# Fifteen unread one-element instructions behind the early sums of a fused decode layer

## The chip, the cores and the metric

The kernel runs on one core of a Trainium2 chip. The metric is the device time of one execution in microseconds (us). A core has five engines, each with a program of its own: TensorE (PE in the profile, PEld for its weight loads), VectorE (DVE), ScalarE (ACT), GpSimd (POOL) and SyncE (SP). [...] An engine's queue is written with a q (DVEq); instructions there, such as semaphore waits and DRAINs, are not counted as busy.

## What is computed

One decode step for 4 sequences with model width 1024, in bf16: a layer norm, grouped-query attention over the last 2048 positions of a key and value cache (32 query heads, 4 key and value heads of 128), a residual, a second layer norm, and a gated feed-forward block of width 3584 with a second residual.

```python
def reference(A_x, A_k_cache, A_v_cache, A_wq, A_wo, B_x, B_w1, B_w3, B_w2):
    x = A_x
    h = x + _A_ref(_layernorm(x, axis=-1), A_k_cache, A_v_cache, A_wq, A_wo)
    ...
    def _B_ref(x, w1, w3, w2):
        gate = jnp.einsum("bsd,df->bsf", x, w1)
        up = jnp.einsum("bsd,df->bsf", x, w3)
        h = _silu(gate) * up
        out = jnp.einsum("bsf,fd->bsd", h, w2)
        return out
    ...
    return h + _B_ref(_layernorm(h, axis=-1), B_w1, B_w3, B_w2)
```

## The kernel before

All weights and the two caches stream from HBM once, through SP's queue, into one large SBUF buffer, `ring` (line 96), whose five units are used over again. The order of the work is written out by hand (`manual_schedule`, line 134): each engine runs its instructions in the order of the program text, and the framework adds the semaphore waits. SBUF tiles that are allocated later lie behind those allocated earlier in the same pool; `ring` lies behind the pool `act`.

The stages are: layer norm of x and the query projection (to line 259); transposes of the keys and the scores (lines 277 to 434); softmax and the weighted values (to line 453); the output projection, whose residual sum lands in `h1`, 128 partitions of 256 numbers (lines 455 to 497); the second layer norm; gate and up projections (line 505 on); and the down projection with `w2`, which ends the kernel.

The down projection is cut in two by the order in which `w2` arrives. The early part multiplies the first 21 of 28 row groups and one part of the last into `early_ps` (function `early`, L560, and L583). Then VectorE adds `early_ps` to `h1` in two sums, one for each half of the partitions (L596); these are the two early sums of the title. The late part multiplies the remaining groups into three accumulators `y2_ps` (function `late`, L608). One matmul (L627) carries a part of `h1` into the second of them. The end is:

- ScalarE copies a piece of the result out of PSUM (L641) and VectorE adds two others to `h1` (L642 and L646). Each of L642 and L646 waits for its early sum and for TensorE.
- SP and ScalarE send two pieces each to HBM (L651).
- The closing block of the program, all on L679: SP waits for the output DMAs and for the last count of each engine's semaphore. Then come two barriers. In each, every engine but GpSimd executes a DRAIN that also counts up a gather semaphore, and then waits for a release; GpSimd executes a DRAIN of its own, waits for the four reports and releases all. Between the two barriers GpSimd clears the semaphores (EVENT_SEMAPHORE_RANGE_CLEAR). A DRAIN starts only when the release semaphore of the barrier before is back at zero. The opening block (L668) has one such barrier.

Ahead of the change GpSimd's last instruction is L542, a product for the last row group, and VectorE's are the two sums of L596.

Of the kernel before, what the change touches and what calls it, by code (L numbers as in the profile page):

```python
# [10 lines left out]
P = 128  # L11
# [4 lines left out]
FP32 = mybir.dt.float32  # L16
# [5 lines left out]
def kernel(  # L22
# [20 lines left out]
    nc = tc.nc  # L43
# [41 lines left out]
    act = ctx.enter_context(tc.tile_pool(name="act", bufs=1))  # L85
# [56 lines left out]
    for b in range(B):  # L142
# [19 lines left out]
        out=same[:], in_=t32[:].rearrange("p (o h) -> p o h", o=1).to_broadcast([P, C, R])  # L162
# [16 lines left out]
        out=asel[:].rearrange("p a y -> p y a"), in0=fold2[:, :, 0], in1=fold2[:, :, 1], op=ALU.add  # L179
# [3 lines left out]
    for j in range(JM):  # L183
# [3 lines left out]
        out=nscale[:], in_=ident_f[:2, :2], scalar=-qscale, op=ALU.mult  # L187
# [5 lines left out]
        out=place[:, : R * C].rearrange("p (h e) -> p h e", e=C)[:, :, C - 1], in_=t32[:]  # L193
# [6 lines left out]
        out=gather[:, :, :B], in_=ident[:].rearrange("p (c b s) -> p c b s", c=C, b=B)[:, :, :, 0]  # L200
# [60 lines left out]
    for r in range(REP):  # L261
# [8 lines left out]
        out=Qm[:].rearrange("p b (g y) -> p b g y", y=QW)[:, :, :, :REP],  # L270
        in_=qT_ps[:, :, :, :B].rearrange("p r g b -> p b g r"),
# [223 lines left out]
    h1 = act.tile([P, DQ], FP32)  # L495
# [42 lines left out]
    for hf in range(2):  # L538
# [4 lines left out]
        out=last_m[:],  # L543
# [50 lines left out]
    for k in range(2):  # L594
        part = h1[2 * R * k : 2 * R * k + 2 * R, :]
        nc.vector.tensor_tensor(out=part, in0=early_ps[:, k], in1=part, op=ALU.add)  # L596

    y2_ps = [
        ps.tile(shape, FP32, tag=tag, name="y2_ps")
        for shape, tag in (([P, DH], "scA"), ([P, DH], "ktB"), ([P, DQ], "scB"))  # L600
# [37 lines left out]
    for k in range(2):  # L638
        part = slice(2 * R * k, 2 * R * k + 2 * R)
        if k == 0:  # L640
            nc.scalar.copy(out=res[part, DH:], in_=y2_ps[1][part, :])  # L641
            nc.vector.tensor_tensor(  # L642
                out=res[part, :DH], in0=y2_ps[0][part, :], in1=h1[part, :DH], op=ALU.add
            )
        else:
            nc.vector.tensor_tensor(  # L646
                out=res[part, :], in0=y2_ps[2][part, :], in1=h1[part, :], op=ALU.add
            )
        for i, eng in enumerate((nc.sync, nc.scalar)):
            c = 2 * k + i  # L650
            eng.dma_start(  # L651
                out=out_flat[:, c * DQ : (c + 1) * DQ], in_=res[R * c : R * c + B, :]
# [31 lines left out]
```

## Time and profile before

| | us |
|---|---|
| median of 3 runs (lowest to highest) | 138.51 (138.48 to 138.62) |
| the profiled execution | 138.48 |
| its span, first to last instruction | 136.7 |
| TensorE busy | 80.7 (59%) |
| VectorE busy | 48.6 (36%), 45 instructions |
| GpSimd busy | 17.7 (13%), 50 instructions |
| HBM read | 55.58 MB, 407 GB/s over the span |

Times inside the profile are counted from the start of the span. Where a record is given to the thousandth, it is read from the trace's own start and length of that instruction; the views print starts to a tenth or a hundredth. A line of the groups reads: line, engine, operation, output and input with shapes, count, then busy us and mean ns of one, then the idle time of the engine just before and what ended it. Matmul ends are modelled, and GpSimd's spans are rough.

### The profile page before, as it was taken

What the parts mean: (1) busy time and instruction counts of PE and PEld (TensorE: products, weight loads), DVE (VectorE), ACT (ScalarE), POOL (GpSimd) and SP (SyncE); (2) the same over time, 40 slices, a digit from 0 to 9 for tenths busy, and PEclk for the clock granted to TensorE, in tenths of its full rate; (3) what the DMA queues carried; (4) which work ended last, traced back from release to release, by engine and by line L of the source; (5) the groups of instructions that cost most, each with busy time, mean ns of one, the idle gap of its engine ahead of it and who ended that gap; (6) DMA issues with size and microseconds to landing.
All of it is one profiled execution on the core that took longest, in us unless ns stands there. A gap on an engine that the chain in (4) does not pass through costs nothing.

```text
span 136.7 us, 1804 instructions
## 1 busy us (share of the span) xinstructions
PE 80.7 (59%) x779; PEld 43.5 (32%) x779; DVE 48.6 (36%) x45; ACT 29.9 (22%) x35; POOL 17.7 (13%) x50
## 2 busy tenths in 40 slices
PE   0000044959999985129992993995198000999770
PEld 0000022449966941023332340541043000444440
DVE  0000110007625463899299922001100297062022
ACT  3000140027959495013000000002501700000100
POOL 7600061000000000000084633000300000001000
PEclk9999999999999999855698699999856855569998
DMA  4999697999999999998978979969899798999960
GB/s 168 525 420 538 269 537 307 436 417 446 417 422 441 412 432 422 417 590 360 556 326 384 537 326 475 520 285 537 352 453 508 302 520 364 397 414 423 403 235 2
DMA packets 2782, 55.69 MB, mean 407 GB/s; under 512 B 312, under 2 KB 600, under 8 KB 728
## 3 DMA queue, kind: packets, MB, share of 16 engines
q1 hardware_dynamic: 2740, 55.58, 95.3%
q8 instruction: 6, 0.10, 0.3%
q10 hardware_dynamic: 36, 0.01, 0.0%
HBM read 55.58 MB, written 0.01 MB: 407 GB/s over the span
## 4 chain that ended last, share of the span: by engine, by line
DMA 56%; PE 30%; DVE 6%; ACT 3%; SPq 1%; issue 1%; DVEq 0%
DMA ring<-in_B_w_dram 40%; DMA ring<-in_A_wq_dram 16%; PE kt_ps L283 9%; PE sc_ps L306 5%; PE o_ps L397 5%; PE gate L510 4%; PE q_ps L249 4%; DVE P L360 2%; DVE PT L382 2%; SPq L128 1%; ACT ring L287 1%; PE small L397 1%; DVE ring L285 1%; DVE rmax L318 1%; ACT q_sb L259 1%
## 5 line engine op out<-in xcount | busy, mean ns | idle before, releaser
L287 ACT COPY ring<-kt_ps 128x2048 bf16<-128x2048 bf16 x8 | 14.6, 1866 | 7.1 <-PE kt_ps L283 7.1
L283 PE MATMUL kt_ps<-ident,ring 128*128 128x128 bf16 x256 | 15.0, 219 | 0.6 <-DVE Qm L269 0.5
L283 PEld LDWEIGHTS <-ring 128*128 128x128 bf16 x256 | 14.4, 98 | 2.6 <-issue 1.7
L414 POOL TENSOR_TENSOR o<-od 128x256 f32<-128x256 f32 x4 | 6.8, 1696 | 55.5 <-DVE od L405 55.5
L285 DVE COPY ring<-kt_ps 128x2048 bf16<-128x2048 bf16 x8 | 9.8, 1225 | 9.3 <-PE kt_ps L283 9.3
L510 PE MATMUL up<-ring,n_T 128*32 128x448 bf16 x64 | 6.0, 568 | 10.9 <-DMA ring<-in_B_w_dram 10.9
L209 PE MATMUL sums_ps<-both,mean_f 128*128 128x64 f32 x4 | 1.1, 366 | 19.0 <-ACT both L207 19.0
L397 PE MATMUL o_ps<-ring,PT 128*128 128x512 bf16 x32 | 11.5, 541 | 0.0
L510 PEld LDWEIGHTS <-n_T 128*32 128x32 bf16 x128 | 5.1, 143 | 20.3 <-DMA ring<-in_B_w_dram 11.5
L397 PEld LDWEIGHTS <-PT 128*128 128x128 bf16 x64 | 7.6, 121 | 10.3 <-issue 5.7
L532 DVE RECIPROCAL eg<-eg 128x896 f32<-128x896 f32 x1 | 5.8, 5753 | 10.9 <-ACT eg L531 10.9
L360 DVE TENSOR_TENSOR P<-p,gmask 128x2048 bf16<-128x2048 bf16 x4 | 9.1, 2278 | 0.8 <-ACT p L347 0.8
L382 DVE STREAM_TRANSPOSE PT<-P 128x2048 bf16<-128x2048 bf16 x4 | 9.2, 2306 | 0.1
L249 PE MATMUL q_ps<-ring,n_T 128*32 128x512 bf16 x64 | 6.2, 556 | 3.6 <-DMA ring<-in_A_wq_dram 1.8
L306 PE MATMUL sc_ps<-ring,Qm 128*32 128x512 bf16 x64 | 7.6, 605 | 0.4 <-DVE ring L285 0.4
L510 PE MATMUL gate<-ring,n_T 128*32 128x448 bf16 x64 | 5.9, 558 | 3.0 <-DMA ring<-in_B_w_dram 3.0
L397 PE MATMUL small<-ring,PT 128*128 128x512 bf16 x32 | 7.2, 379 | 0.0
L484 PE MATMUL y_ps<-ring,oP 128*32 128x512 bf16 x64 | 7.1, 379 | 0.1
L209 PEld LDWEIGHTS sums_ps<-both,mean_f 128*128 128x128 f32 x4 | 0.8, 249 | 19.4 <-issue 17.1
L234 DVE STREAM_TRANSPOSE x_T<-x_nat 128x256 bf16<-128x256 bf16 x1 | 0.6, 626 | 15.9 <-DMA x_nat<-in_A_x_dram 15.9
L560 PE MATMUL early_ps<-ring,hg_T 128*32 128x512 bf16 x42 | 5.0, 379 | 1.1 <-DMA ring<-in_B_w_dram 1.1
L464 ACT CAST oP<-on_ps 128x128 bf16<-128x128 f32 x1 | 0.3, 266 | 22.6 <-PE on_ps L457 22.6
(94 smaller groups left out, 68.9 us busy)
## 6 DMA issues: line engine op xcount, KB each, us to landing
ring<-in_B_w_dram SPq DMA_DIRECT2D x2, 7168.0 KB
ring<-in_A_k_cache_dram SPq DMA_DIRECT2D x4, 2048.0 KB, 25.6
ring<-in_A_v_cache_dram SPq DMA_DIRECT2D x4, 2048.0 KB, 42.8
ring<-in_A_wq_dram SPq DMA_DIRECT2D x1, 7168.0 KB, 21.2
ring<-in_B_w_dram SPq DMA_DIRECT2D x1, 3328.0 KB
ring<-in_B_w_dram SPq DMA_DIRECT2D x1, 2048.0 KB, 23.3
ring<-in_A_wq_dram SPq DMA_DIRECT2D x1, 1024.0 KB, 4.5
ring<-in_B_w_dram SPq DMA_DIRECT2D x1, 1024.0 KB
```

The lines of the kernel that those rows point to most:

```text
L249: nc.tensor.matmul(q_ps[R * c : R * c + R, hf], lhsT=xn_T[:, kc, :], rhs=wq_s[:, kc, o : o + HALF * Dh], start=(kc == 0), stop=(kc == KC - 1),
L283: nc.tensor.transpose(out=kt_ps[:, jj], in_=blocks[:, jj, :], identity=ident[:])
L285: nc.vector.tensor_copy(out=blocks, in_=kt_ps[:])
L287: nc.scalar.copy(out=blocks, in_=kt_ps[:])
L306: nc.tensor.matmul(sc_ps[b // 2][R * q : R * q + R, b % 2], lhsT=Qm[:, b, g * R : (g + 1) * R], rhs=kT[:, b, g, q], start=(g == 0), stop=( ...
L360: nc.vector.tensor_tensor(out=P4[:], in0=stage.pop(("p1", b))[:].rearrange("p (x o) -> p x o", o=1).to_broadcast([P, JR * L5, Hkv]), in1=g ...
L382: nc.vector.transpose(out=PT[:].rearrange("p j h -> p (j h)"), in_=stage.pop(("P4", b))[:].rearrange("p x g -> p (x g)"),)
L397: nc.tensor.matmul(o_ps, lhsT=PT[:, i * JM : (i + 1) * JM, :].rearrange("p j h -> p (j h)"), rhs=v_s[b][:, i * JM : (i + 1) * JM, :], star ...
L414: nc.gpsimd.tensor_tensor(out=o2[:], in0=od[:, :2], in1=od[:, 2:], op=ALU.add)
L484: nc.tensor.matmul(y_ps[R * i : R * i + R], lhsT=oP[:, t, :], rhs=row[:, i], start=False, stop=(t == T - 1), tile_position=(0, R * i), ski ...
L510: nc.tensor.matmul(out_ps[hf][R * c : R * c + R, :], lhsT=hn_T[:, kc, :], rhs=cols[:, kc, c, hf], start=(kc == 0), stop=(kc == KC - 1), ti ...
L532: nc.vector.reciprocal(out=eg[:], in_=eg[:])
```

## The change

Two tiles of 128 by 8 fp32 are allocated in the pool `act`, one for each engine. Behind the two early sums GpSimd copies one element of `h1` into its tile, and then seven further elements of each tile are set to zero, VectorE writing its own and GpSimd its own. Nothing reads the two tiles. Lines behind the insertion have numbers higher by 7: L642 becomes L649, L646 becomes L653, L679 becomes L686.

```diff
@@ -595,6 +595,13 @@
         part = h1[2 * R * k : 2 * R * k + 2 * R, :]
         nc.vector.tensor_tensor(out=part, in0=early_ps[:, k], in1=part, op=ALU.add)
 
+    pad_v = act.tile([P, 8], FP32)
+    pad_p = act.tile([P, 8], FP32)
+    nc.gpsimd.tensor_copy(out=pad_p[:1, :1], in_=h1[:1, :1])
+    for i in range(1, 8):
+        nc.vector.memset(pad_v[:1, i : i + 1], 0.0)
+        nc.gpsimd.memset(pad_p[:1, i : i + 1], 0.0)
+
     y2_ps = [
         ps.tile(shape, FP32, tag=tag, name="y2_ps")
         for shape, tag in (([P, DH], "scA"), ([P, DH], "ktB"), ([P, DQ], "scB"))
```

In the built programs VectorE has 67 instructions in the body in place of 60 and GpSimd 62 in place of 54; TensorE, ScalarE and SP have as many as before, in the same order with the same waits. The one new wait is that of GpSimd's copy for the second early sum; SP's closing wait asks for 54 counts of GpSimd's semaphore in place of 46. The seven memsets of VectorE stand ahead of the waits of L649 in its program. The buffer `ring` starts 64 bytes higher in each partition, as does `res`, the tile of the result.

## The prediction, made before the result was known

> **What bounds the kernel now.** I read the page's chain first, then the timeline of the last 6 us, then the records of the closing line L679, which the chain leaves out. The chain says that the weight stream sets the pace:
>
> ```profile
> DMA 56%; PE 30%; DVE 6%; ACT 3%; SPq 1%; issue 1%; DVEq 0%
> ```
>
> The change lies behind the last big wait on that stream. The timeline from 131 us (start, length, engine, line; in brackets the idle time before it and what ended it):
>
> ```profile
> 131.04 0.87 DVE L596 TENSOR_TENSOR h<-early_ps,h 64x256 f32<-64x256 f32 x2 [7.06 <-PE early_ps L560]
> 131.61 0.63 PE L608 MATMUL y_ps<-ring,hg_T 128*32 128x128 bf16 x24 [0.60 <-DMA ring<-in_B_w_dram]
> ...
> 132.17 0.43 PE L627 MATMUL y_ps<-h,ident_f 128*64 128x128 f32 x2
> ...
> 132.88 0.62 PE L608 MATMUL y_ps<-ring,hg_T 128*32 128x128 bf16 x14 [0.28 <-DMA ring<-in_B_w_dram]
> 133.26 0.28 DVE L642 TENSOR_TENSOR res<-y_ps,h 64x128 bf16<-64x128 f32 x1 [1.35 <-PE y_ps L608]
> ...
> 133.58 0.43 DVE L646 TENSOR_TENSOR res<-y_ps,h 64x256 bf16<-64x256 f32 x1
> ```
>
> The two early sums (L596) end at 131.91. VectorE then stands idle for 1.35 us, until TensorE's late products, which themselves wait for the last weights, release L642. GpSimd does nothing after L542 ends at 124.68.
>
> The span ends at 136.69, 2.7 us after L646. Output DMAs take it to 135.64; then come two closing barriers, in which every engine reports with a DRAIN, GpSimd gathers the reports, and all are released. The records of L679 from 135.6 to 136.8 (engine's queue, count, ns min/median/max, first and last start):
>
> ```profile
> L679 SPq DRAIN  x2: 7/7/7, 135.6 to 135.9; - x2
> ...
> L679 POOLq DRAIN  x2: 39/58/78, 135.8 to 136.1; - x2
> L679 ACTq DRAIN  x1: 8/8/8, 135.9 to 135.9; - x1
> L679 POOLq EVENT_SEMAPHORE_RANGE_CLEAR  x1: 96/96/96, 135.9 to 135.9; - x1
> L679 PEldq DRAIN  x1: 13/13/13, 136.0 to 136.0; - x1
> L679 DVEq DRAIN  x1: 143/143/143, 136.3 to 136.3; - x1
> ```
>
> All four other engines are released by the first barrier at about 135.80. SP starts its next DRAIN 75 ns after its release has ended, ACT 74, PE 98; VectorE needs 496 ns (135.825 to 136.321), and its DRAIN lasts 143 ns where VectorE's own DRAIN at the program's start took 10. GpSimd has finished its own duties at 136.107, and its gather comes at 136.498, 34 ns behind the end of VectorE's DRAIN (136.464). So **VectorE holds up the last barrier**, by 0.35 us over what GpSimd would need (136.107 + 0.044, the spacing of GpSimd's DRAIN and gather in the opening barrier, is 136.15). Nothing that the trace records as a wait explains this: the semaphore that the DRAIN asks to be zero is zero when PE's release ends, 135.855, and SP and ACT pass at once.
>
> **My reading of it.** The late instruction is a place in VectorE's program rather than a kind of work. Instructions reach the engines in pieces, as page part 3 shows:
>
> ```profile
> q8 instruction: 6, 0.10, 0.3%
> ```
>
> That is 0.10 MB in 6 packets, some 16 KB each, during the span, for the engine with the long program. VectorE's built program has 3 instructions in the opening block, 60 in the body and 4 at the end; the slow one is the 66th, the second closing DRAIN. I take it that a boundary between pieces lies there and costs 0.43 + 0.13 = 0.56 us (the late start over 75 ns, the long DRAIN over 10 ns). That is an inference: the trace holds one such place on VectorE.
>
> [...]
>
> **The change part by part.**
>
> *Removed and moved.* Nothing is taken out. TensorE, ScalarE and SP keep their instructions and waits in the same order. On VectorE all that follows L596 moves 7 places down: the 66th instruction is now the semaphore wait ahead of the first result sum (L642, now L649), right behind the last memset. The boundary, if it is one, is then passed in the 1.35 us of idle time, and the closing DRAIN is an ordinary one. VectorE would report at 135.825 + 0.09 + 0.01 = 135.93, GpSimd gathers at 136.15 in place of 136.498: **-0.35 us**. What is late next is GpSimd itself.
>
> *Seven memsets on VectorE.* The trace has no memset on VectorE. The nearest rows:
>
> ```profile
> L341 DVE COPY bias<-small 128x2 f32<-128x2 f32 x2 | 0.3, 133 | 1.3 <-PE small L333 1.3
> L378 DVE RECIPROCAL rinv<-small 128x2 f32<-128x2 f32 x2 | 0.3, 131 | 0.0
> ...
> L184 POOL MEMSET jmask<- 32x1 f32 x4 | 0.4, 91 | 0.2
> ...
> L668 POOL MEMSET const-float32-0.0<- 128x1 f32 x1 | 0.1, 98 | 0.2 <-issue 0.2
> ```
>
> Upper end: 133 ns and the 31 ns between the two L596 make 164, times 7 is 1.15 us. Lower end: GpSimd's four opening memsets start 34 ns apart, times 7 is 0.24. I take the same kind of operation's length, 98 ns: 0.69 us, from 131.91 to 132.60. Add 0.56 for the boundary: 133.16, before TensorE's release at 133.24. So **0 us**. The spare time is only 0.08 us, but VectorE's sequencer runs ahead: L642's first wait is recorded at 131.497, during the second L596, so the stall can begin while the memsets still run. At the upper end VectorE would be ready at 133.62, 0.36 us late, which eats the whole gain; at the lower it has 0.5 us to spare. Neither TensorE's L627 nor anyone else waits for the memsets.
>
> *Eight instructions on GpSimd.* The copy waits for the second L596 and reads one element of its result. The smallest such rows take 200 ns (L171, L199). Seven memsets start 34 ns apart (L668) to 128 ns (L184): 0.24 to 0.90. From 131.94 they end between 132.4 and 133.05. Behind them GpSimd has only the closing barrier, whose first gather waits for SP at 135.64: 2.6 us of cover, so **0 us**. SP's closing wait asks for eight more counts from GpSimd, long there.
>
> *Do the two disturb one another?* The rows that bear on it are GpSimd's sums beside a busy and beside an idle VectorE:
>
> ```profile
> 68.94 2.70 POOL L414 TENSOR_TENSOR o<-od 128x256 f32<-128x256 f32 x1 [47.97 <-DVE od L405]
> ...
> 80.67 0.73 POOL L414 TENSOR_TENSOR o<-od 128x256 f32<-128x256 f32 x1 [3.32 <-DVE od L405]
> ```
>
> The first runs beside VectorE's L360 (68.77 to 71.05), the second alone: GpSimd lost 2 us, VectorE nothing (L360 took 2.28 us there and 2.29 without GpSimd). So GpSimd yields, and it has cover.
>
> [...]
>
> *Memory.* The two pads push the weight buffer up by 64 bytes in each partition; packet sizes stay. No row prices this. A tenth of a percent of the 136.7 us of streaming would be 0.14 us either way; I take 0.
>
> **Sum.** The profiled execution took 138.48 us, 1.79 more than its span, and lies 0.03 below the median 138.51. 138.48 - 0.35 = 138.13, or 138.16 against the median: I say **138.15**.
>
> **The rivals.**
>
> *No change.* VectorE's late DRAIN belongs to the closing sequence itself (whatever comes second there is late) and moves along. For it: a single observation, and none of VectorE's 65 earlier instructions can be seen to stall, though most lie behind longer waits. Against it: no other engine is late at that step, and VectorE's opening DRAIN took 10 ns. Everything added is covered: 138.5.
>
> *Slower: the boundary lands in a worse place.* If the real boundary lies up to 7 places past the 66th, today it falls behind the span's last release; moved 7 up, it falls in the closing barriers, where VectorE is already last, at up to 0.56 us: 139.05. Or the memsets cost so much that the stall ends past 133.24. That decides from 0.11 us per memset on, and outweighs the saving from about 0.16. At that upper end the first result sum is 0.36 us late and the gain is gone; only beyond it is the change a loss. For it: each late step of VectorE now has something ahead of it. Against: the late DRAIN sits where a boundary would show.
>
> *Slower: GpSimd holds VectorE up.* Should all 15 run one after another at upper prices, 1.15 + 0.2 + 0.9 = 2.25 us from 131.91 is 134.16, 0.9 us past 133.26, less 0.35 at the end or not: 139.0 to 139.4. The L414 rows speak against it.
>
> *GpSimd has a late place of its own* between 136.107 and 136.464, now hidden, and its 8 instructions fail to move it away: the gain shrinks to below 0.2, counted as no change.
>
> **How the numbers follow.** About 0.2% (0.28 us) is what a measurement of this kernel can tell from no change. Forecast (faster by 0.25%): 0.50, a little of it falling below that line by the memsets' price, against some chance that more is saved in the 1.79 us outside the span. No change, with the shrunken gain: 0.28. The boundary in a worse place: 0.16; GpSimd holding VectorE: 0.06. So faster 0.50, same 0.28, slower 0.22. The forecast's own range is 137.95 to 138.30 (0.35 with the 0.14 of the buffer's shift); the range of all, to 138.85, takes in no change and the milder losses, and leaves out some 0.15.
>
> **What would show it.** Right: VectorE's last DRAIN starts within 0.1 us of its release, lasts some 10 ns, and the gather follows GpSimd's own DRAIN; the memsets end before 132.7; the first result sum still starts 20 to 30 ns after TensorE's last FIRST product. Wrong: the DRAIN is as late as before (no change), L649 starts later against TensorE than 0.03 us (boundary or memsets too dear), or the closing barriers grow. The forecast fails as a whole if the delay follows the closing sequence and not the count of instructions.

## The result, and the profile after

The changed kernel is **slower by 0.51%** (ratio 1.0051, 95% interval 1.0032 to 1.0070): median 139.15 us over 14 executions (138.78 to 140.12) against 138.63 (138.48 to 138.80). The prediction was 138.15. Seven of the 14 lie at 138.97 or below and seven at 139.33 or above, and the median is the middle between the two groups; the profiled one took 138.93, with a span of 137.12 where the span before was 136.69.

The end of the timeline of the changed kernel (start, length, engine, line, in brackets the idle time and what ended it):

```profile
129.94 1.90 PE L560 MATMUL early_ps<-ring,hg_T 128*32 128x512 bf16 x16 [1.71 <-DMA ring<-in_B_w_dram]
...
131.88 0.87 DVE L596 TENSOR_TENSOR h<-early_ps,h 64x256 f32<-64x256 f32 x2 [8.06 <-PE early_ps L560]
132.36 0.18 POOL L600 COPY pad_p<-h 1x1 f32<-1x1 f32 x1 [7.85 <-DVE h L596]
...
132.48 0.29 POOL L603 MEMSET pad_p<- 1x1 f32 x7
132.80 0.11 DVE L602 MEMSET pad_v<- 1x1 f32 x7
...
133.67 0.61 PE L615 MATMUL y_ps<-ring,hg_T 128*32 128x128 bf16 x14 [0.28 <-DMA ring<-in_B_w_dram]
...
134.06 0.28 DVE L649 TENSOR_TENSOR res<-y_ps,h 64x128 bf16<-64x128 f32 x1 [1.15 <-PE y_ps L615]
```

Three things are to be seen. The fifteen instructions are short and covered: VectorE's seven take 0.11 us, GpSimd's eight 0.41, and VectorE still waits for TensorE before L649. Everything is late *before* they start: the early sums begin at 131.88 where they began at 131.04. And what came late is a weight load: TensorE waited 1.71 us for its rows ahead of 129.94. Before the change the same products stood here:

```profile
129.10 1.90 PE L560 MATMUL early_ps<-ring,hg_T 128*32 128x512 bf16 x16 [0.76 <-DMA ring<-in_B_w_dram]
```

The closing barrier, on the other hand, is as short as predicted. The records of the closing line from 136.7 to 136.97:

```profile
L686 DVEq DRAIN  x1: 19/19/19, 136.7 to 136.7; - x1
...
L686 POOLq DRAIN  x1: 34/34/34, 136.9 to 136.9; - x1
L686 POOLq EVENT_SEMAPHORE  x1: 17/17/17, 136.9 to 136.9; - x1
```

VectorE's last DRAIN now starts 90 ns after its release and lasts 19 ns (496 and 143 before); the last gather follows GpSimd's own DRAIN. From the first release to the last gather it is 0.38 us in place of 0.73. So the account of the profiled execution is **+0.79 us** on the weight stream, **-0.35** at the closing barrier, together +0.44; the spans differ by 0.43.

What is new in the page is one row of part 3. The rows behind the weight queue's, before and after:

```profile
q8 instruction: 6, 0.10, 0.3%
q10 hardware_dynamic: 36, 0.01, 0.0%
```

```profile
q8 instruction: 6, 0.10, 0.3%
q10 hardware_dynamic: 36, 0.01, 0.0%
q14 instruction: 2, 0.02, 0.0%
```

Two pieces of program, 8 KB each, are now fetched inside the span. The list of packets has them at 103.37 and 120.08 us; before, two such packets came at 136.99 and 137.18, behind the span's end. The weight queue and the fetch in the window 119.8 to 121 (packets, MB, share of 16 engines):

```profile
q1 hardware_dynamic: 22, 0.59, 116.9%
q14 instruction: 1, 0.01, 1.7%
```

Here is how so small a packet can matter. Each of the large loads lands in 16 parts, which I read as one for each of the core's 16 DMA engines (no view names the engine of a part), and TensorE starts behind the last: the parts of the 8 rows land by 129.06 before and by 129.90 after, the products on them start at 129.10 and 129.94. The landing times of the parts, from the trace, in us after the first part of the same load (13 rows of w2 at 122.3, then 8 rows at 127.2; between them lies the small load of 128 KB for the last row group, L524):

```
            13 rows: early parts   late parts            8 rows: late parts
before      11, 0.00 to 0.50       1.71 1.80 1.83 1.86 1.86           nine, 1.62 to 1.87
after       9, 0.00 to 0.36        0.73 1.25 1.59 ... 1.77 (five)     1.54 ... 1.77 (seven), 2.20, 2.74
```

Five parts are late by 1.59 us or more at 122 in both kernels: by then five 16 KB pieces have been fetched (the packets of queue 8, which I take for TensorE's, the engine with the long program: 779 products and 779 weight loads; no view names the engine). The small load makes four more late. In the changed kernel two further parts stand out at 122, by 0.73 and 1.25, and behind the small load they stand at 2.20 and 2.74: **they gained another 1.47 and 1.49**. So, if a part is a DMA engine, each fetch fell on one that the small load makes late as well, and the delays added up. The four parts of the small load itself show the same: before, they land within 0.12 us of one another; after, two of them land 0.67 and 1.20 us behind the first (with VectorE's instructions alone, in the experiments, one of the four does, by 1.23; with GpSimd's alone one, by 0.65). The later loads keep that order, and the last part of the last 512 KB load lands at 133.63 in place of 132.84.

### The profile page after: what moved, and what is told of

It reads as the page before. It is cut to its first block, busy times and chain, and to the rows that moved or that the text cites. A ratio compares the mean times of both kernels' runs of the same rounds, so it can differ in the third digit from the quotient of the medians.

```text
span 137.1 us, 1817 instructions
## 1 busy us (share of the span) xinstructions
PE 80.1 (58%) x777; PEld 43.3 (32%) x779; DVE 48.8 (36%) x52; ACT 29.9 (22%) x35; POOL 18.2 (13%) x58
## 4 chain that ended last, share of the span: by engine, by line
DMA 56%; PE 30%; DVE 6%; ACT 3%; SPq 1%; issue 1%; DVEq 0%
DMA ring<-in_B_w_dram 41%; DMA ring<-in_A_wq_dram 15%; PE kt_ps L283 9%; PE sc_ps L306 5%; PE o_ps L397 4%; PE gate L510 4%; PE q_ps L249 4%; DVE P L360 2%; DVE PT L382 2%; SPq L128 1%; ACT ring L287 1%; PE small L397 1%; DVE ring L285 1%; DVE rmax L318 1%; ACT q_sb L259 1%
```

## The experiments

My theory (A in the texts below) was now: the longer programs of VectorE and GpSimd have their next piece fetched during the stream, and the fetch makes one DMA engine late. The rivals were the weight buffer's 64 bytes (B), and the instructions themselves (C). All kernels allocate the two tiles, and the diffs below are against the changed kernel, unless the text says otherwise.

### One engine at a time

```diff
-    nc.gpsimd.tensor_copy(out=pad_p[:1, :1], in_=h1[:1, :1])
     for i in range(1, 8):
         nc.vector.memset(pad_v[:1, i : i + 1], 0.0)
-        nc.gpsimd.memset(pad_p[:1, i : i + 1], 0.0)
```

> Both tiles allocated, VectorE's seven memsets kept, GpSimd's eight instructions left out. Theory A (an engine whose program grows past a boundary fetches its next piece of program during the weight stream, and the fetch holds up the one DMA engine that carries it): one packet of 8 KB on queue 14 inside the span in place of two, VectorE's second closing DRAIN starts within 0.1 us of its release and lasts some 20 ns, the last weights land either as before (time 138.25) or up to 0.8 us late (139.0). Theory B (the 64-byte shift of the weight buffer slows the stream): as slow as the whole change less nothing, 139.0 to 139.2, with no packet needed. Theory C (the 15 instructions disturb each other or the end): about 138.6.

```diff
     for i in range(1, 8):
-        nc.vector.memset(pad_v[:1, i : i + 1], 0.0)
         nc.gpsimd.memset(pad_p[:1, i : i + 1], 0.0)
```

> Both tiles allocated, GpSimd's eight instructions kept, VectorE's memsets left out. Theory A: one packet on queue 14 inside the span, VectorE's closing DRAIN as late as before (0.5 us after its release, 143 ns long), so the end saves nothing; time 138.6 if the fetch falls on a DMA engine with time to spare, up to 139.4 if not. Theory B: 139.0 to 139.5. Theory C: about 138.6.

VectorE alone: 139.60 us (ratio 1.0064, 1.0043 to 1.0085). GpSimd alone: 138.91 (1.0036, 1.0018 to 1.0055). Each has one packet in the stream, so the fetches can be told apart: VectorE's is the one at 120 us, GpSimd's the one at 101 to 103. The queue's row in the window 119.8 to 121 of VectorE alone, then in 101 to 102 of GpSimd alone:

```profile
q14 instruction: 1, 0.01, 1.7%
```

```profile
q14 instruction: 1, 0.01, 1.9%
```

The last part of the 512 KB load lands at 133.62 and 133.19. VectorE alone was dearer than expected, because its closing barrier saves nothing: GpSimd has a late place of its own. The closing line from 137.25 to 137.85 in that kernel:

```profile
L684 POOLq DRAIN  x1: 39/39/39, 137.4 to 137.4; - x1
L684 POOLq EVENT_SEMAPHORE  x1: 17/17/17, 137.8 to 137.8; - x1
```

VectorE has reported at 137.24, yet GpSimd gathers 0.40 us after its own DRAIN (137.415 to 137.813), where the opening barrier needs 0.044. Before the change that was hidden behind VectorE, but with nothing to spare: there GpSimd's gather stood 0.39 us behind its own DRAIN too (136.107 to 136.498). So there were two late places that ended together. From the first release to the last gather it is 0.73 us before, 0.74 with VectorE's instructions alone, 0.74 with GpSimd's alone (there VectorE's DRAIN is the late one, 126 ns long), and 0.38 only with both.

### The tiles without instructions, and the instructions in another place

```diff
     pad_v = act.tile([P, 8], FP32)
     pad_p = act.tile([P, 8], FP32)
-    nc.gpsimd.tensor_copy(out=pad_p[:1, :1], in_=h1[:1, :1])
-    for i in range(1, 8):
-        nc.vector.memset(pad_v[:1, i : i + 1], 0.0)
-        nc.gpsimd.memset(pad_p[:1, i : i + 1], 0.0)
```

> The two tiles are allocated and nothing is done with them: the weight buffer starts 64 bytes higher, the programs are those of before. Theory A: 138.6, no packet on queue 14 inside the span, closing DRAIN as late as before. Theory B: 139.0 to 139.5, the last weights land 0.4 to 0.8 us later. Theory C: 138.6.

The other kernel has the seven and the eight ahead of the first transpose, at line 238, and nothing behind the early sums (against the kernel before):

```diff
+    pad_v = act.tile([P, 8], FP32)
+    pad_p = act.tile([P, 8], FP32)
+    for i in range(1, 8):
+        nc.vector.memset(pad_v[:1, i : i + 1], 0.0)
+    for i in range(8):
+        nc.gpsimd.memset(pad_p[:1, i : i + 1], 0.0)
+
     x_T = act.tile([P, KC, R], BF16, tag="xT")
```

> As many instructions as in the whole change (seven memsets on VectorE, eight on GpSimd), but at the head of the kernel, where VectorE waits 15 us for its first input and GpSimd prepares constants; none stands behind the early sums. Theory A (the count decides, not the place): two packets on queue 14 inside the span, a short closing DRAIN on VectorE, the same time as the whole change within 0.3 us (138.8 to 139.5). Theory B: the same 139.0 to 139.5. Theory C (disturbance at the end): 138.6 or below.

The tiles alone: 138.43 us, ratio 0.9985 (0.9977 to 0.9994), no packet, closing DRAIN late as before. The 64 bytes cost nothing; this kernel is a little faster than the one before: B falls. At the head: 138.96 (1.0040, 1.0022 to 1.0059), two packets (103.5 and 118.0 us), a short closing DRAIN: C falls too. **With these counts it is the number of instructions that decides, not their place.**

### The small load over all DMA engines

```diff
-    load(w2_a, w2_v[:, FC - 1, :HD].rearrange("(y a) n -> a y n", a=C))
+    load(w2_a, w2_v[:, FC - 1, :HD].rearrange("(p t) n -> p t n", p=PA))
```

> The whole change, and the small load of the last row group (128 KB, which goes to HBM's and SBUF's sides in 4 outer rows and was carried by 4 of the 16 DMA engines) written with 16 outer rows, so that all 16 carry it; the rows then lie in another order, so a small part of the last group's products is not the reference's. Theory A (each of the two fetches falls on a DMA engine that the small load makes late as well, and the two delays add up): two packets on queue 14 inside the span, but no part of the last loads stands out by more than 0.3 us; the last weights land at most 0.4 us later than in the spread kernel without the fifteen instructions, or at the same time, and this kernel is 0.3 to 0.4 us faster than that one by the shorter closing barrier: about 138.3 to 138.6. Theory D (a fetch costs the stream its delay whatever else its DMA engine carries): 0.4 to 0.8 us slower than that kernel, 139.2 or more.

> The two tiles alone, none of the fifteen instructions, and the small load of the last row group over all 16 DMA engines as in the kernel beside it (the same part of the output is not the reference's). Theory A: no packet on queue 14 inside the span, VectorE's closing DRAIN late; the DMA engines that carried TensorE's program pieces are late by their 1.3 us and now by some 0.3 us of the small load too, so the last weights land 0.2 to 0.4 us later than with the tiles alone: 138.6 to 138.8. Theory D: the same.

With the fifteen instructions 139.77 us (1.0089, 1.0076 to 1.0102), without them 140.16 (1.0123, 1.0097 to 1.0148). The order is that of A, and so is the distance: 0.39 us faster with them by the medians, though the two intervals just overlap. The last part of the 512 KB load lands at 134.50 with and 134.54 without, so two fetches in the stream (101.4 and 119.1 us) cost nothing there, and from the first release to the last gather it is 0.38 us with and 0.74 without. D falls. The level was missed by 1.2 and 1.4 us: with 16 outer rows the small load, whose target is still only 16 partitions, made *every* part of the loads behind it about 1.7 us later, where with four it made four parts 1.5 us later. Why, these runs do not show.

That 4 outer rows mean 4 DMA engines, and 16 all of them, is my reading. The trace has the number: before the change the small load lands in 4 parts (123.91 to 124.03 us), and behind it nine parts of a large load are late in place of five. Which engines carry a fetch, no view here names, but by the late parts of the small load they are among its four.

### How the late place moves with the count

```diff
     nc.gpsimd.tensor_copy(out=pad_p[:1, :1], in_=h1[:1, :1])
-    for i in range(1, 8):
+    for i in range(1, v + 1):
         nc.vector.memset(pad_v[:1, i : i + 1], 0.0)
+    for i in range(1, p):
         nc.gpsimd.memset(pad_p[:1, i : i + 1], 0.0)
```

Here v is the number of memsets on VectorE and p that of GpSimd's instructions, the copy included; the kernels write the same instructions out or in another order of the two engines, and each engine's own order is this one. With v = 3, p = 4, and with v = 1, p = 1:

> Three memsets on VectorE and four instructions on GpSimd in place of seven and eight. If both programs pass the boundary with so few: two packets on queue 14 inside the span and the time of the whole change, 138.8 to 139.9. If one passes: one packet, 138.9 to 139.6. If neither: no packet, 138.4 to 138.6, or 138.1 if the closing DRAIN is short all the same, which my prediction's count of places allows (the late place would then fall behind the last result sum, where VectorE waits for the first closing release).

> One memset on VectorE and the one copy on GpSimd. If a boundary is passed by so little: packets on queue 14 inside the span as above, 138.8 or more. If not: 138.4 with the closing DRAIN as late as before, or 138.1 with a short one (by the count of places, the late place would fall on VectorE's wait for the first closing release, where 1.7 us are free).

3 and 4: 139.36 us (1.0058, 1.0046 to 1.0070). 1 and 1: 138.63 (1.0004, 0.9996 to 1.0013). No packet comes in the stream in either, the last weights land as with the tiles alone (132.74, 132.70; there 132.78), and the late place sits where the count puts it. With one memset VectorE's closing DRAIN is short (24 ns, 135.81), but GpSimd's one instruction brings its late place onto its last DRAIN (371 ns after the clearing, 176 long; the last gather at 136.53), where nothing hides it. With three VectorE's falls on the second result sum, which starts 0.23 us behind the first, and GpSimd's on the first release, 0.40 us behind the gather:

```profile
133.16 0.28 DVE L652 TENSOR_TENSOR res<-y_ps,h 64x128 bf16<-64x128 f32 x1 [1.19 <-PE y_ps L618]
...
133.68 0.43 DVE L656 TENSOR_TENSOR res<-y_ps,h 64x256 bf16<-64x256 f32 x1 [0.23 <-DVE res L652]
```

The rest of its loss is a longer wait for the output, which I put down to a fetch that meets it; no run separates the two. VectorE's packet comes at 134.33, among the four output pieces, and SP's wait for them (us in total, times, longest) is 0.7 us longer than before. The wait before, then here:

```profile
SPq L679 <- DMA out_dram<-res: 1.0, 2, 0.7
```

```profile
SPq L689 <- DMA out_dram<-res: 1.7, 2, 1.4
```

The stalls with 0 and with 3 memsets put the place at the 64th instruction of VectorE's program, if the two block branches, of which the trace has no record, are left out of the count; with 1 and 7 nothing contradicts it. GpSimd's stalls with 0, 1 and 4 instructions (gather, DRAIN, first release) fit one place too.

### A count that hides both places

By these counts one memset puts VectorE's place on its wait for the first release, and five instructions put GpSimd's on its wait for the first reports. Four more kernels: v = 1, p = 5; v = 1, p = 6; v = 5, p = 7; and 1 and 5 with GpSimd's five (all memsets) at the head of the kernel, as in the diff for the head above. Theory E, in the texts, is that any lengthening of a program costs.

> One memset on VectorE, one copy and four memsets on GpSimd behind the early sums. Theory A, with the places as the runs so far have them (each added instruction moves the late place one instruction towards the front): VectorE's late place falls on its wait for the first closing release, GpSimd's on its wait for the first reports; both have over 1.5 us free. Both closing barriers are then short (0.35 us from the first release's end to the last gather), the last weights land as with the tiles alone, fetches come after them: 138.0 to 138.1. If GpSimd's fetch meets the output pieces (134.2 to 134.9) on one DMA engine, their landing is up to 0.8 us later: 138.9. Theory E (any lengthening costs): 138.6 or more.

> One memset on VectorE, one copy and five memsets on GpSimd behind the early sums. Theory A: GpSimd's late place falls on its own first closing DRAIN, behind the last memset, with 3 us free; fetch some 1.2 us after that or later: 138.0 to 138.1, unless the fetch meets the last weights or the outputs, 138.4 to 138.9. Theory E: 138.6 or more.

> Five memsets on VectorE, one copy and six memsets on GpSimd behind the early sums. VectorE's late place would fall on the first result sum, two instructions ahead of the end of the body; GpSimd's on the last instruction of its body or the first behind it. If a piece whose first instruction still belongs to the body is fetched ahead of need: a packet on queue 14 near 120 us for VectorE, no stall at the first result sum, the last weights 0.5 to 0.9 us late, 138.8 to 139.9. If only seven and eight reach that far: no packet before 131 us, the first result sum starts 0.2 to 0.5 us after TensorE's release, 138.3 to 138.8, or 0.8 more if a fetch meets the outputs.

> One memset on VectorE behind the early sums as before, GpSimd's five instructions as memsets at the head of the kernel. The programs are as long as those with one and five behind the early sums, but GpSimd reaches its closing block at 124.7 and not at 132. Theory A with a fetch that follows the passing of the place: the fetch comes between 125 and 130 us, inside the stream, onto a DMA engine of the small load; the last weights are 0.4 to 0.9 us late, 138.4 to 139.0 (closing barrier short). If the place in the text doesn't matter: the same time as with the five behind the early sums.

| kernel | GpSimd's fetch, us | VectorE's fetch, us | last part of the 512 KB load, us | median, us | ratio (95%) |
|---|---|---|---|---|---|
| 1 and 5 | 132.88 | 135.10 | 132.71 | 138.13 | 0.9964 (0.9951 to 0.9977) |
| 1 and 6 | 101.22 | 135.54 | 133.11 | 138.58 | 1.0024 (1.0000 to 1.0048) |
| 5 and 7 | 101.39 | 134.96 | 133.27 | 139.38 | 1.0050 (1.0037 to 1.0063) |
| 1 and 5, five at the head | 127.27 | 136.45 | 133.34 | 138.59 | 1.0005 (0.9993 to 1.0017) |

**1 and 5 beats both kernels**: 0.48 us below before. Its closing line from 135.82 to 136.1, both places hidden, and the fetch in the window 132.5 to 133.5, behind the last large loads:

```profile
L687 DVEq DRAIN  x1: 24/24/24, 135.8 to 135.8; - x1
...
L687 POOLq EVENT_SEMAPHORE  x1: 17/17/17, 136.1 to 136.1; - x1
```

```profile
q14 instruction: 1, 0.01, 3.3%
q1 hardware_dynamic: 7, 0.00, 1.2%
```

The kernel with the five at the head is the sharpest pair to it: the programs are as long, both barriers as short, but GpSimd is through with its work at 123.7 (the end of its first DRAIN) and not at 131.8, its piece is fetched at 127.27, inside the stream, and not at 132.88, and the last part lands 0.64 us later; the medians differ by 0.46. The fetch in its window 127 to 128, beside a weight queue that is full:

```profile
q1 hardware_dynamic: 41, 0.47, 112.1%
q14 instruction: 1, 0.01, 1.9%
```

For 1 and 6 my expectation was wrong: the piece was fetched at 101 us, long before GpSimd came to the place. For 5 and 7 neither of my two cases came as written: GpSimd's piece was fetched in the stream, VectorE's was not, and the first result sum starts 23 ns behind TensorE's release, as before (24), so no stall shows; 0.66 us of idle time stand ahead of it. E falls with 1 and 5.

Over all kernels with the small load in 4 outer rows the fetch sorts the times of the last weights: in the seven with a piece fetched inside the stream the last part of the 512 KB load lands at 133.10 to 133.63, in the five without at 132.70 to 132.84.

## Why the prediction was wrong

- **What bounds the kernel, and the late DRAIN: right in kind, and half of the account.** That the lateness belongs to a place in VectorE's program, and that seven instructions take it off the DRAIN, is shown by the runs with 0 and 3, where the stall moves, and by those with 1 and 7, where the DRAIN is short. The count was off by two: I called it the 66th instruction and counted the two branches. But "VectorE holds up the last barrier" named one of two late places that ended together. The sum credited the 0.35 us to VectorE's memsets alone, and by themselves these save nothing at the barrier (0.74 us against 0.73). That 0.35 was measured in the whole change is luck: it took GpSimd's eight as well, which the sum put at nothing.
- **"The boundary, if it is one, is then passed in the 1.35 us of idle time": this step failed.** I priced a boundary as a stall of the engine that passes it and quoted the row that shows pieces being fetched, but gave the fetch itself no place in the sum. What comes with the boundary is also a transfer. Before the change it followed the passing by 1.17 us (135.83 to 136.99), out of the way; with seven memsets it came at 120.08, inside the stream, and the last weights landed 0.79 us later. VectorE's seven alone do that (133.62 against 133.63 with both): GpSimd's late part lies behind VectorE's later one.
- **"Eight instructions on GpSimd ... 0 us": wrong for the same reason.** Their run time is covered, as I said; the 8 KB that they move to 103 us is not. By themselves they cost 0.48 us (138.91 against 138.43 for the tiles alone).
- **The memsets' price: too high, and without effect.** I took 0.69 us from GpSimd's length of 98 ns; VectorE starts them 7 to 9 ns apart and has all seven done in 0.11.
- **Memory: a shift of either sign up to 0.14 us** was allowed; the kernel with the tiles alone is 0.2 us (0.15%) faster than the one before.
- **The signs.** All that the prediction named for being right came but one: the DRAIN starts 0.09 us after its release and lasts 19 ns, the gather follows GpSimd's own DRAIN, the first result sum starts 24 ns behind TensorE's release. Only the memsets end later than 132.7, at 132.91, because the sums ahead of them are late. No sign looked at the landing of the weights.
- **The rivals.** "No change", by a DRAIN that is late wherever it stands, falls with the short DRAIN. Slower was forecast with 0.22, by a stall in a worse place or by GpSimd holding up VectorE; neither occurred, so that this rival has the sign of the result is luck. A late place of GpSimd's was named and exists, but the eight instructions did move it away. None of the rivals had a transfer in it.
- **What a place in the program costs.** The row of 16 KB pieces that I quoted is not that of these two engines: theirs are packets of 8 KB on queue 14. The stall is 0.40 us on GpSimd and 0.56 on VectorE where the place falls in the closing barriers, and a piece fetched in the stream makes its part 0.44 us (GpSimd alone) to 0.93 (VectorE alone) later than the next latest.

What stays open. First, when a piece is fetched, and what the stall is. With 7 instructions or fewer from the place to the end of the program (VectorE with 0 to 5, GpSimd with 0 to 5) the packet came once the place was reached (1.0 to 1.4 us after, and 3.5 us with the five at the head), with 8 or more (GpSimd 6 to 8, VectorE 7) 13 to 32 us ahead of it; that is a pattern in fourteen kernels, not an explanation, and VectorE with 6 was not tried. Nor does the stall wait for that packet: before the change VectorE's late DRAIN is over at 136.46, and the packet starts at 136.99. Second, why two packets of the same size cost their DMA engines different delays. Third, why half of the executions of the changed kernel are another 0.4 to 1.2 us longer. Four profiles of the longer executions (VectorE alone, GpSimd alone, 5 and 7, five at the head) show TensorE at half clock in the last stage. The window 130.2 to 133.6 of the change (138.93) and of GpSimd alone (139.50), with the granted clock behind the POOL column:

```profile
130.20:133.60 3.40, 2.63 (x42) 1.46 (x39) 0.94 (x9) 0.00 (x0) 0.41 (x8) 1.00 0.48 184
```

```profile
130.20:133.60 3.40, 3.30 (x37) 1.90 (x34) 0.83 (x2) 0.00 (x0) 0.41 (x8) 0.50 0.49 188
```

In the clock's own records that half-clock stretch lasts 3.4 us in all four and begins at 129.9 to 131.2, behind a wait of TensorE for weights near 128.3 of 1.2 to 1.7 us; before the change that wait is 0.76. Five other profiles have such a wait, of 1.1 to 1.7 us, the changed kernel's among them, and no such stretch. In the changed kernel and the six others whose last weights land at 133.1 to 133.6 the executions spread over 0.6 to 1.7 us; in the five whose last weights land by 132.9, the kernel before among them, over 0.2 to 0.4, but for one execution of 1 and 1 at 141.02. That the lateness brings the lower clock about fits this, but was not tested.

## What to carry to other kernels

An instruction that is hidden on its own engine can still cost: GpSimd's eight were done by 132.77 us in the changed kernel, 3.7 us ahead of the first gather, and by themselves they cost 0.48 us (138.91 against 138.43). They lengthen that engine's program, and the page's rows of kind "instruction" show whether a piece of program is now fetched beside the data. A load was here as late as its slowest part (the 8 rows of the changed kernel: 14 parts by 128.93 us, the last at 129.90, the products at 129.94), so look at how the parts land, and at which small loads and fetches share the late ones, before pricing a few KB at nothing. Where a barrier's reports come late without a wait, count instructions: one memset on VectorE took its late DRAIN from 143 ns to 24, and two kernels that differ by a single padding instruction of GpSimd differ by 0.45 us (138.13 with 1 and 5, 138.58 with 1 and 6).

## What the runs showed that I had not expected

- A packet of 8 KB that takes 0.31 to 0.33 us puts one part of a load about 0.4 to 0.5 us (GpSimd's) or 0.7 to 0.9 us (VectorE's) behind the ordinary ones, and the part stays late to the end of the stream, which in the changed kernel keeps the 16 DMA engines 99% busy from 122 to 130.2 us.
- The six 16 KB pieces of queue 8 (0.9 to 1.1 us each) do the same: behind each, one more part of every load lands 1.5 to 1.9 us after the first, and up to the small load it is these parts that end every large load, in the kernel before as well.
- The load of 128 KB into 16 partitions was dearer with 16 outer rows (all parts of the loads behind it about 1.7 us later) than with four (four parts 1.5 us later): 140.16 us against 138.43 without the fifteen instructions.
- Seven one-element memsets on VectorE start 7 to 9 ns apart; on GpSimd they start 31 to 35 ns apart.
- Two late places, one on VectorE and one on GpSimd, held the last barrier up to the same moment (0.73 us with both, 0.74 with either), so that taking one away showed nothing.
